# Pair sums kept in SBUF, V in P's tiles, mixed weights stored split, transfers counted by the planner

## The chip, the cores and the metric

One core of a Trainium2 chip. The metric is the device time of one execution in microseconds, the median of several runs. TensorE multiplies; VectorE (DVE), ScalarE (ACT) and GpSimd (POOL) do the elementwise work; SP issues most DMA transfers, GpSimd and ScalarE some.

## The reference

The input x has 2048 rows of 640. Two branches are mixed by a gate per row, `g = sigmoid(sum(x * gate_w))`:

```python
out = g * A(x) + (1 - g) * B(x)
# A: 32 heads of 20, 4 segments of 512 rows, causal softmax attention inside a segment,
#    plus a memory of the segments before it
for s in range(4):
    p = softmax(qs @ ks.T * scale + mask);  a_dot = p @ vs
    a_mem = (phi(qs) @ M) / (phi(qs) @ z + 1e-6)        # phi(t) = t + 1 if t > 0 else exp(t)
    o = sigmoid(beta) * a_mem + (1 - sigmoid(beta)) * a_dot
    M += phi(ks).T @ vs;  z += sum(phi(ks))
A = o @ wo
# B: a gated feed-forward layer with 1728 hidden columns
B = (silu(x @ w1) * (x @ w3)) @ w2
```

All is float32.

## The kernel before, in words

**Precision.** A float32 operand is split into a high and a low part, both in the type that TensorE multiplies at full rate; a product is three passes, high by high, high by low, low by high (`PASSES`). The function `split` makes such a pair: ScalarE casts (L194), then DVE or GpSimd subtracts (L189).

**TensorE in halves.** Most products are cut into two halves of 64 rows of the contraction, which run side by side in the array. The first halves of a product (`Work`) are issued first; at the end of them SP gets a no-operation that waits for TensorE (`w.seen`, L288), and the first matmul of the second half waits for that no-operation. So SP, which also issues transfers in order, stands in TensorE's way whenever a transfer ahead of the no-operation waits.

**The order of work is written out by a planner in the source.** `clocks` are planned TensorE times of the two halves, `busy` the planned ends of the other engines, `heap` things due later. Durations in it are constants (600 ns for a ScalarE pass, `LAND` 4200 ns for a store to land, `AGE` 5000 ns for a weight). `braid(a, b, every, skip)` runs a stream b beside a: one step of b each `every` ns of TensorE work, after `skip` ns. `segs` gives each stage of dense work and the attention slot at which it ends; attention (`attention`) runs through all stages beside the dense work.

**Stages.** The head projects Q, V and K of the first two chunks (a chunk is a segment) and writes the memory of both. Then stages of dense work beside attention: the feed-forward of pair A (chunks 0 and 1), its down products with the output projection of chunk 0; the projections of chunks 2 and 3 with the output projection of chunk 1; the feed-forward of pair B (chunks 2 and 3); its down products and the rest.

**Feed-forward of a pair.** `ffn_pair` multiplies two chunks by two weights with seven products where eight would be plain: it needs sums of blocks of x (`S`, four sums for each of two blocks k) and mixtures of the weights w1 and w3 (`mix`). `store_sums` computes the sums of both pairs in the head: it loads blocks of x into the tile `sx`, four additions each, splits each sum and stores both parts to DRAM (`sd`). `load_sums` loads them again at the pair: six into the two slots of the tag `acc` (after the memory writes that read V there; for pair B, after the third memory read and the whole output of chunk 1), two into the X tile of the second chunk. The mixtures of the weights are made once, for pair A, and stored unsplit to `md` (three per column block j, 13 blocks); pair B loads them into raw tiles (`w_load`) and splits them again (`w_split`) into the eight weight tiles `W`.

**After-steps of a product** (`after_w`, `after_3`, `after_4`) add, take tanh and multiply. They work in the product's PSUM bank where they can, so the bank is held for two or three operations.

**Tiles that matter here.** `acc`: two wide slots, first raw x, then V of chunks 0 and 1, then sums of pair A, then accumulators. `P32`: two tiles, first raw weights, then the exponentials P of attention. `hT`, `f`: rings of short-lived tiles.

**Attention.** For each pair of heads: scores (`s`), row maxima on DVE, the maxima turned and sent by GpSimd's DMA into two rows of the q tile (`row_in`, qk<-mr), then scores again with the maximum subtracted (`t`, L1491), exponentials on ScalarE (L1498), masks on GpSimd, and P times V (`o`).

Of the kernel before, what the change touches and what calls it, by code (L numbers as in the profile page):

```python
# [20 lines left out]
P = 128  # L21
# [11 lines left out]
NP, AGE = 2, 5000  # L33
# [9 lines left out]
COL, COL4, MIN_MM, APART, ISSUE, AHEAD = 0.4533, 1.7, 62, 5, 580, 1500  # L43
# [3 lines left out]
LAND, SPARE, EVEN, NOP = 4200, 99999, 0, 80  # L47
# [4 lines left out]
def gated_mix(ctx: ExitStack, tc: tile.TileContext, xT, wqk, wv, w13, w2, w2h, wo, beta, out):  # L52
# [11 lines left out]
    md = dp.tile([NF, 3, P, D], F32, name="md")  # L64
# [71 lines left out]
    busy, heap = dict(act=0.0, dve=0.0, pool=0.0, sp=0.0), []  # L136

    def now():
        return max(clocks)

# [339 lines left out]

    def slot(name):
        return cp.tile([P, 6 * L], F32, tag="acc", name=name, bufs=2)
# [34 lines left out]
    def w_load():  # L517
        k = clock["next"]
        src, n, queue, needs, *_ = items[k]
# [5 lines left out]
        if k in EARLY:  # L525
            if k % 2 == 0:
                early[:] = [sp.tile([P, 2, 1280], F32, tag="P32", name=f"wr{k}", bufs=NP)]
# [4 lines left out]
        queue.dma_start(raw[:, :n], src)  # L532
        t = go(*(("pool", ISSUE) if queue is nc.gpsimd else ("sp", 400)))
        raws.append([k, raw, n, t + AGE])
        clock["next"] += 1
        kind = items[k][6]
        if kind is not None:
            kind[1].append(raw)
            if len(kind[1]) == 2:
                for i in range(2):  # L540
                    raws.append([k + 1 + i, kind[1][i], D, t + AGE])
                clock["next"] += 2

    def w_split():
# [31 lines left out]
    def mix(w, ri, rj, j, k, done):  # L576
# [13 lines left out]
        def after():  # L590
            for i, (x, n) in enumerate(((t, 2 * P), (ri, D), (rj, D))):
                store_later(md[j, i, :, :n], x[:, :n], ("m", j, i))
# [10 lines left out]
    def w_step():  # L603
# [8 lines left out]
        if clock["next"] < min(len(items), limit() + NRAW) and landed.issuperset(items[clock["next"]][3]) and \  # L612
# [3 lines left out]
    def w_get(i):  # L616

        while i not in tiles:
# [11 lines left out]
            elif not raws or raws[-1][0] < i and clock["raws"] - len(freed) < NRAW:  # L630
# [141 lines left out]
    def store_later(dst, src, key=None, queue=nc.sync, t=None, done=None):  # L772
# [3 lines left out]
        def issue():  # L776
# [5 lines left out]
            later(go(e, 400 if e == "sp" else 330) + LAND, land)  # L782
# [142 lines left out]
    def v_blocks(c, iv, end):  # L925
# [3 lines left out]
        def begin_v():  # L929
            big["v", c] = V = slot(f"V{c}")[:, :4 * H * VE].rearrange("p (l h e) -> p l h e", l=4, e=VE)  # L930
# [182 lines left out]
    def store_sums():  # L1113

        w = cp.tile([P, KB, L], F32, tag="oall", name="sx", bufs=1)
        free_at = [0.0] * KB
        rounds = [(cs, k) for cs in ((0, 1), (2, 3)) for k in range(2)]
        loads = [(n, i) for n in range(4) for i in (2, 1, 0, 3)]
        at = {}

        def beat():
            if loads and min(free_at) <= now():
# [6 lines left out]
                store_later(w[:, slot_], xT[d, :, kb, :], ("s", n, i))  # L1129
# [22 lines left out]
        for n, (cs, k) in enumerate(rounds):  # L1152
            while not all(("s", n, i) in landed for i in range(4)):
# [12 lines left out]
            for m, o in ((2, 0), (3, 1), (1, 2), (4, 3)):  # L1166
                while not room("f", 2):
# [6 lines left out]
        selection()  # L1174

    def load_sums(cs):

        c, e = cs
        S = sums[cs] = {}

        def free_slots():
            return all((k, b) in Ms for b in range(KB) for k in cs if k < NSEG - 1) and \
                (not c or read.count(3) == 8 and all(("out", 1, q) in landed for q in range(4)))
# [4 lines left out]
        while not free_slots():  # L1188
            yield 1
        a, b = [cp.tile([P, 2, 3, L], FR, tag="acc", name=f"S{c}_{i}", bufs=2) for i in range(2)]  # L1190
        for m, k, home in ((2, 0, a[:, :, 0]), (2, 1, a[:, :, 1]), (3, 0, a[:, :, 2]), (3, 1, b[:, :, 0]), (1, 0, b[:, :, 1]), (1, 1, b[:, :, 2])):
            while ("S", cs, m, k) not in landed:
                yield 1
            load(m, k, home)
            yield 1
        while e in halves_left or not {("S", cs, 4, k) for k in range(2)} <= landed:
            yield 1
        for k in range(2):
            load(4, k, Xs[e][:, :, k])
            yield 1  # L1200
# [3 lines left out]
    def plan_pair(j, again):  # L1204

        if again:
            return [w_add(w13[2 * j], D, even=True), w_add(md[j, 0, :, :2 * P], 2 * P, even=True, needs=[("m", j, 0)]),
# [827 lines left out]
```

## Time and profile before

| | us |
|---|---|
| median of 3 runs | 1135.32 (1133.02 to 1136.27) |
| the profiled execution | 1138.12 |
| its span, first to last instruction | 1136.4 |
| TensorE busy | 1090.8 (96%) |
| DVE, ScalarE, GpSimd busy | 706.0, 563.0, 528.4 |
| mean granted TensorE clock | 0.978 |

The DMA engines moved 224.47 MB, 198 GB/s in the mean. Busy time of TensorE is the time in which at least one matmul is under way; two halves that run side by side count once, and a half that runs alone counts as busy too. A row "A <- B: total, times, longest" says that A's engine waited for B. In a chain or a timeline, `SPq` is SP's queue; the line behind it says which code issued.

### The profile page before, as it was taken

The page shows a single profiled execution, that of the slowest core. Times are in us where ns is not written, and L with a number is a line of the kernel's source. Part 1 is how long each engine was busy: PE and PEld are TensorE (multiplying, and loading weights), DVE is VectorE, ACT ScalarE, POOL GpSimd, SP SyncE. Part 2 cuts the span into 40 slices and gives each one's busy share as a digit, 9 for nine tenths or more (in the row PEclk, how much of TensorE's full clock was granted, in tenths as well). Part 3 has the DMA queues.
Part 4 walks back from the last instruction along what each step waited for, and adds up shares of the span by engine and source line. Part 5 has one row for each costly group of instructions (what it writes and reads, how often), then busy time and mean ns, then how long its engine had stood idle before and what let it go on. Part 6 is the DMA issues. An engine that isn't in the chain of part 4 may idle for free.

```text
span 1136.4 us, 29929 instructions
## 1 busy us (share of the span) xinstructions
PE 1090.8 (96%) x11369; PEld 976.3 (86%) x11369; DVE 706.0 (62%) x1932; ACT 563.0 (50%) x1158; POOL 528.4 (46%) x744
## 2 busy tenths in 40 slices
PE   9989889999999999999999998999999999999998
PEld 7978768878798899899889977878998778999998
DVE  6255457777766667575456666636767666764552
ACT  6255333554555564464766562425555545565220
POOL 3142445563446445357566573415444554545130
PEclk9999899999999999999999998969999999999999
DMA  9697795665656765556788596665576584754541
GB/s 317 223 318 273 240 348 169 185 196 166 184 173 181 215 182 162 163 151 191 233 250 274 165 316 206 194 218 154 154 197 173 140 224 120 198 150 126 170 155 48
DMA packets 145831, 224.47 MB, mean 198 GB/s; under 512 B 23148, under 2 KB 70424, under 8 KB 145688
## 3 DMA queue, kind: packets, MB, share of 16 engines
q1 hardware_dynamic: 113848, 164.73, 45.6%
q0 software_dynamic: 24064, 43.68, 15.4%
q10 hardware_dynamic: 7776, 14.16, 3.4%
q8 instruction: 90, 1.47, 0.6%
q14 instruction: 53, 0.43, 0.1%
HBM read 133.73 MB, written 87.82 MB: 195 GB/s over the span
## 4 chain that ended last, share of the span: by engine, by line
PE 77%; DMA 8%; POOL 5%; issue 4%; ACT 2%; SPq 2%; DVE 2%; POOLq 0%; DVEq 0%; ACTq 0%
PE f L285 17%; PE c L285 13%; PE z L285 6%; PE op L285 6%; PE v L285 6%; PE o L1524 6%; PE k L285 4%; PE w L285 4%; PE q L285 4%; PE t L1491 3%; PE s L1429 3%; DMA qk<-mr 3%; POOL W L189 2%; DMA sd<-S 2%; PE g L285 1%
## 5 line engine op out<-in xcount | busy, mean ns | idle before, releaser
L1440 DVE CUSTOM_DVE_ANT_0 junk<-s,mask 128x128 bf16<-128x128 f32 (+3 forms) x512 | 251.0, 490 | 138.1 <-PE s L1429 95.3
L189 POOL TENSOR_TENSOR W<-wr,W 128x640 fp32r<-128x640 f32 (+3 forms) x129 | 200.4, 1561 | 173.1 <-ACT W L194 159.4
L1498 ACT ACTIVATE P<-t 128x384 f32<-128x384 f32 (+1 forms) x384 | 180.9, 528 | 127.2 <-PE t L1491 111.2
L285 PE MATMUL c<-X,W 64*128 64x512 f32 x936 | 233.9, 399 | 0.0
L1507 POOL TENSOR_SCALAR_AFFINE_SELECT P<-P 128x256 f32<-128x256 f32 (+1 forms) x192 | 97.2, 516 | 238.6 <-ACT P L1498 212.6
L285 PE MATMUL c<-S,W 64*128 64x512 f32 x624 | 180.6, 406 | 3.3 <-DMA S<-sd 3.3
L194 ACT CAST W<-wr 128x640 fp32r<-128x640 f32 (+2 forms) x218 | 149.0, 704 | 51.7 <-PE f L285 23.4
L285 PEld LDWEIGHTS c<-X,W 64*128 64x128 f32 x936 | 155.8, 188 | 7.7 <-issue 1.4
L285 PE MATMUL f<-XW,W 64*128 64x320 f32 x1536 | 156.1, 308 | 2.6 <-SPq L288 2.6
L285 PEld LDWEIGHTS f<-XW,W 64*128 64x128 f32 x1536 | 148.2, 185 | 3.9 <-SPq L288 2.8
L285 PE MATMUL f<-W,W 64*128 64x320 f32 x1056 | 131.0, 310 | 0.2 <-SPq L288 0.2
L285 PE MATMUL w<-X,W 64*128 64x512 f32 x468 | 129.1, 396 | 0.0
L285 PE MATMUL z<-X,W 64*128 64x512 f32 x468 | 128.9, 396 | 0.0
L285 PEld LDWEIGHTS c<-S,W 64*128 64x128 f32 x624 | 116.1, 190 | 8.7 <-DMA S<-sd 3.7
L1491 PE MATMUL t<-qk 62*128 62x256 f32 (+2 forms) x512 | 108.0, 336 | 11.6 <-DMA qk<-mr 8.9
L285 PEld LDWEIGHTS f<-W,W 64*128 64x128 f32 x1056 | 113.5, 185 | 1.7 <-issue 0.6
L285 PE MATMUL k<-X,W 64*128 64x512 f32 x600 | 114.2, 412 | 0.4 <-SPq L288 0.4
L1429 PE MATMUL s<-qk 60*128 60x256 f32 (+2 forms) x512 | 107.2, 331 | 3.3 <-DMA qk<-qkd 1.3
L285 PE MATMUL q<-X,W 64*128 64x512 f32 x480 | 90.5, 413 | 6.4 <-SPq L288 6.4
L285 PE MATMUL op<-W,oT 64*128 64x320 f32 x960 | 93.7, 308 | 0.5 <-DVE oT L189 0.4
L285 PE MATMUL v<-W,X 64*128 64x322 f32 (+2 forms) x948 | 92.8, 309 | 0.1
L285 PEld LDWEIGHTS op<-W,oT 64*128 64x128 f32 x960 | 88.9, 185 | 2.1 <-DVE oT L189 1.3
(157 smaller groups left out, 2153.8 us busy)
## 6 DMA issues: line engine op xcount, KB each, us to landing
qk<-qkd POOLq DMA_DIRECT2D x128, 240.0 KB, 4.9
wr<-in_w_dram SPq DMA_DIRECT2D x69, 320.0 KB
hd<-H SPq DMA_DIRECT2D x26, 512.0 KB
qkd<-qs SPq DMA_DIRECT2D x20, 512.0 KB
qkd<-ks SPq DMA_DIRECT2D x20, 512.0 KB
wr<-hd SPq DMA_DIRECT2D x32, 320.0 KB
md<-wr SPq DMA_DIRECT2D x26, 320.0 KB
wr<-md SPq DMA_DIRECT2D x26, 320.0 KB
```

What stands on the lines that cost most here:

```text
L189: return lambda: e.tensor_sub(dst[:, 1], src, dst[:, 0].bitcast(F32))
L194: stages(bank, ("act", ns, lambda: nc.scalar.copy(dst[:, 0], src)), low, done=done)
L285: ins = nc.tensor.matmul(o, l, x, start=not w.more and i == 0 and (r == 0 or not w.todo[0]), stop=i == len(todo) - 1 and (r == 1 or not w. ...
L1429: nc.tensor.matmul(ps[i][:, o:o + n], q[:, qb * P:(qb + 1) * P], k[:, :n], start=qb != 1, stop=qb != 0, skip_group_check=True)
L1440: nc.vector.tensor_tensor_reduce(out=junk[:, :n], in0=ps[i][:, o:o + n], in1=mask[:, L - n:], scale=1.0, scalar=-3.0e38, op0=ALU.add, op1= ...
L1491: nc.tensor.matmul(ps[i][:, o:o + L - q0], k[:, kb * P:(kb + 1) * P], q[:, q0:], start=kb != 2, stop=kb != 3, skip_group_check=True)
L1498: nc.scalar.activation(u["P"][:, i, o:o + n], ps[i][:, b:b + n], AF.Exp, scale=SCALE)
L1507: nc.gpsimd.affine_select(d, d, pattern=[[0, 2], [0, n], [1, P]], base=0, channel_multiplier=-1, compare_op=ALU.is_ge, fill=0.0)
L1524: nc.tensor.matmul(ps[32 * i:32 * i + 32, kb * P:], heads[2 * p + i]["v"][:, kb], pairs[p + i // 2]["P"][:, i % 2, o:o + n], start=kb == 0 ...
```

## The change

- **Pair A's sums in place.** `store_sums` runs once for each pair. For pair A it runs in the head, beside V and K, and splits sums 1 to 3 of both blocks straight into the two `acc` slots; only sum 4 goes through DRAM. For pair B it runs beside the last down products of pair A, and all sums go through DRAM as before. `load_sums` of pair B waits for each slot alone: the first after the third memory read, the second after the output of chunk 1. Sum 4's loads are cut by part and not by block.
- **V in P's tiles.** V of chunks 0 and 1 takes the `P32` tiles.
- **Two mixed weights stored split** (`WHOLE`): of the three mixtures the two wide ones are split for pair A as before, and the split pair is stored, 640 KB and not 320; pair B loads it straight into a `W` tile, with no cast and no subtraction.
- **Transfers queued in the planner's clock** (`moved`, `RATE` 320 bytes per ns): each planned landing is at least when the bytes ahead of it have passed. The row transfer is planned at 3800 ns and not 2700.
- **Other after-steps in pair B** (`SOFT`): the sum goes into an SBUF tile, so the bank is free after the first operation (the second in `after_4`); the last multiplication goes to DVE or GpSimd.
- **Stages shifted:** other spacings in `braid`, other stage ends, `AHEAD` 500 and not 1500, `gates` after the first job of the head.

```diff
+NP, AGE, WHOLE, SOFT = 2, 5000, (1, 2), ((2, 0), (2, 1), (2, 2))
-COL, COL4, MIN_MM, APART, ISSUE, AHEAD = 0.4533, 1.7, 62, 5, 580, 1500
+COL, COL4, MIN_MM, APART, ISSUE, AHEAD = 0.4533, 1.7, 62, 5, 580, 500
-    md = dp.tile([NF, 3, P, D], F32, name="md")
+    md = dp.tile([NF, 3, P, 2 * D], F32, name="md")
...
+    def moved(ap, since=None):
+        n = 4
+        for x in ap.shape:
+            n *= x
+        busy["dma"] = max(busy["dma"], now()) + n / RATE
+        return busy["dma"] + 2500
...
+    def p_tile(name, n=2560):
+        t = sp.tile([P, 4 * H * VE], F32, tag="P32", name=name, bufs=NP)
+        return t[:, :n].rearrange("p (h n) -> p h n", h=2)
...
     def w_load():
+        if kind == "whole":
+            w = sp.tile([P, 2, D + 2], FR, tag="W", name=f"W{k}", bufs=NW)
+            halfway.add(k)
+            dst = w[:, :, :n].bitcast(F32)
+            queue.dma_start(dst, src)
+            later(max(go("sp", 400) + AGE, moved(dst)), lambda: (tiles.__setitem__(k, w), halfway.remove(k)))
+            clock["next"] += 1
+            return
...
         def done():
             tiles[k] = w
+            if kind is not None and kind - 1 in WHOLE:
+                store_later(md[items[k][6][2], kind - 1].rearrange("p (a n) -> p a n", a=2), w[:, :, :D].bitcast(F32), ("m", items[k][6][2], kind - 1))
...
+        if clock["next"] < len(items) and items[clock["next"]][6] == "whole":
+            if clock["next"] < limit() and landed.issuperset(items[clock["next"]][3]):
+                w_load()
...
-            big["v", c] = V = slot(f"V{c}")[:, :4 * H * VE].rearrange("p (l h e) -> p l h e", l=4, e=VE)
+            big["v", c] = V = (slot(f"V{c}")[:, :4 * H * VE] if c > 1 else p_tile(f"V{c}", 4 * H * VE).rearrange("p h n -> p (h n)")).rearrange(
+                "p (l h e) -> p l h e", l=4, e=VE)
...
+    SUMS = (((2, 0), (2, 1), (3, 0)), ((3, 1), (1, 0), (1, 1)))
-    def store_sums():
+    def store_sums(cs, first):
+        if first:
+            S = sums[cs] = {}
+            homes = [cp.tile([P, 3, 2, L], FR, tag="acc", name=f"S{cs[0]}_{i}", bufs=2) for i in range(2)]
+            homes = {mk: homes[i][:, n] for i, three in enumerate(SUMS) for n, mk in enumerate(three)}
...
+                if first and m < 4:
+                    def here_(m=m, k=k, n=n, o=o):
+                        S[m, k] = homes[m, k]
+                        free_at[at[n, o]] = now()
+                    split(homes[m, k], x[o], None, 600, here_, spare=EVEN)
...
+        def free_slot(i):
+            return all(("out", 1, q) in landed for q in range(4)) if i else read.count(3) == 8
...
+                if (c, 0) in SOFT:
+                    stages(bank, ("dve", 690, lambda: nc.vector.tensor_add(u, u, ps), True),
+                           ("act", 600, lambda: nc.scalar.activation(t, u, AF.Tanh, scale=0.5)),
+                           ("both", 690, lambda: nc.vector.scalar_tensor_tensor(t, t, 1.0, u, op0=ALU.add, op1=ALU.mult)),
+                           done=lambda: (let(name("a")), ready.add("r")))
...
-        later(t + 2700, lambda: u.update({"in": u.get("in", 0) + 1}))
+        later(max(t + 3800, moved(src) - 500), lambda: u.update({"in": u.get("in", 0) + 1}))
...
-    head += [braid(chain([v1] + jobs_k(A) + job_q(A, 2)), presums, 400, 0, False)]
+    head += [braid(chain([v0, v1] + jobs_k(A) + job_q(A, 2)), (0, store_sums(A, True)), 300)]
...
-    seg = [braid(braid(braid(chain(q + [half, up]), chain([(0, load_sums(A))]), 400, 0), presums, 400, 0), job_read(1), 3800, 11000)]
+    seg = [braid(braid(chain(q + [half, up]), chain([(0, load_sums(A))]), 400, 0), job_read(1), 4400, 17000)]
...
-    seg = [braid(chain([d0, d1]), o1, 1400, 3000), o2, (0, load_raw(2)), braid(chain([d1b, d2]), xs, 2700, 3400, False)]
+    seg = [braid(chain([d0, d1]), o1, 300, 3000), o2, (0, load_raw(2)), braid(braid(chain([d1b, d2]), (0, store_sums(B, False)), 1500, 0), xs, 2700, 3400, False)]
...
-    segs.append((2 * H - 3, seg))
+    segs.append((2 * H - 5, seg))
...
-    segs.append((3 * H + 8, seg))
+    segs.append((3 * H + 9, seg))
```

The spacings of the later stages change likewise (job_read of chunk 2 from 2000 to 2900, of chunk 3 from 2000 and 2400 to 1700, 3200, 3600 and 3300, the output projections from 1800, 1200, 2400 and 1400 to 900, 900, 4200 and 3200).

More of the change, by code (lines that the diff above doesn't have):

```diff
@@ L526, in w_load @@
             if k % 2 == 0:
-                early[:] = [sp.tile([P, 2, 1280], F32, tag="P32", name=f"wr{k}", bufs=NP)]
+                early[:] = [p_tile(f"wr{k}")]
             raw = early[0][:, k % 2]
@@ L532, in w_load @@
         queue.dma_start(raw[:, :n], src)
[L533 to L534 removed]
+        t = max(go(*(("pool", ISSUE) if queue is nc.gpsimd else ("sp", 400))) + AGE, moved(raw[:, :n]))
+        raws.append([k, raw, n, t])
         clock["next"] += 1
@@ L629, in w_get @@
                 clocks[0] = now()
-            elif not raws or raws[-1][0] < i and clock["raws"] - len(freed) < NRAW:
+            elif clock["next"] <= i and (not raws or items[clock["next"]][6] == "whole" or clock["raws"] - len(freed) < NRAW):
                 w_load()
@@ L1152, in store_sums @@
         for n, (cs, k) in enumerate(rounds):
-            while not all(("s", n, i) in landed for i in range(4)):
+            while not all(("s", cs, n, i) in landed for i in range(4)):
                 yield beat()
@@ L1406, in load_pair @@
             go("pool", ISSUE)
+            moved(qkd[c][RH * (h + i):RH * (h + i + 1)])
         if h % 8 == 0:
@@ L1485, in t_unit @@
         if t == 0:
-            u["P"] = sp.tile([P, 2, 1280], F32, tag="P32", name=f"P{p}", bufs=NP)
+            u["P"] = p_tile(f"P{p}")
         banks, ps = zip(*[bank_tile(f"t{p}_{t}_{i}") for i in range(2)])
@@ L1935, in gated_mix @@
     o1, o2 = jobs_oproj(3)
-    tail = [braid(chain([d1b, d2]), o1, 1400, 6000), o2]
+    tail = [braid(chain([d1b, d2]), o1, 3200, 0), o2]
     def at_job(n):
```

88 lines of the change are left out of this document (51 added, 37 removed).

## The prediction

> **What bounds the kernel now.** I read the page's busy lines first, then the busy table cut at the kernel's stages, then TensorE's waits.
>
> ```profile
> span 1136.4 us, 29929 instructions
> PE 1090.8 (96%) x11369; PEld 976.3 (86%) x11369; DVE 706.0 (62%) x1932; ACT 563.0 (50%) x1158; POOL 528.4 (46%) x744
> ```
> The table by stage has the window, its length, the busy time and count of TensorE, weight loads, DVE, ScalarE and GpSimd, the granted clock, the DMA share and GB/s:
> ```profile
> 75.00:175.00 100.00, 84.26 (x742) 74.51 (x740) 53.46 (x109) 40.39 (x80) 37.60 (x58) 0.91 0.86 294
> 175.00:375.00 200.00, 196.97 (x1820) 172.58 (x1817) 147.51 (x435) 104.75 (x216) 104.16 (x149) 1.00 0.60 174
> 375.00:550.00 175.00, 172.19 (x2181) 160.12 (x2180) 113.50 (x329) 94.45 (x193) 92.02 (x125) 1.00 0.64 186
> ...
> 675.00:760.00 85.00, 78.10 (x688) 63.87 (x687) 47.67 (x148) 31.33 (x69) 32.38 (x50) 0.86 0.74 231
> 760.00:980.00 220.00, 211.75 (x1961) 186.74 (x1961) 155.74 (x451) 118.55 (x246) 108.70 (x155) 0.99 0.60 163
> ```
> And TensorE's waits: total us, times, longest.
> ```profile
> PE t L1491 <- DMA qk<-mr: 8.9, 7, 2.6
> PE q L285 <- SPq L288: 6.4, 3, 5.6
> PE pm L285 <- SPq L288: 3.5, 2, 3.3
> PE c L285 <- DMA S<-sd: 3.3, 1, 3.3
> ...
> PE pm L285 <- ACT pkn L1003: 2.7, 1, 2.7
> PE gt L283 <- DMA gm<-gd: 2.3, 2, 1.3
> PE pkt L283 <- SPq L288: 2.1, 2, 1.1
> ```
>
> TensorE is the bound: its matmuls are 96% busy, no other engine is above 62%, and these stages have it 96% busy or more, except two. From 75 to 175 us (the head: K projections, memory of pair A, pair sums) it idles 100 - 84.26 = 15.7 us at a granted clock of 0.91, and there the DMA engines are 0.86 busy, the most of any row. From 675 to 760 us (opening of pair B) it idles 6.9 us at 0.86. Between 175 and 375 us it idles 3.0 of 200 us at 1.00, so 1.5% is what a good stage costs. A change that touches DVE, ScalarE or GpSimd alone moves nothing here; one that takes away idle TensorE time gains that time and the slow clock behind it.
>
> **Step 1, sums of pair A in place; sums of pair B moved out of the head.** The head's waits are named SPq L288: the second row half's first matmul waits for a no-operation on SP, and SP had transfers ahead of it. The rows show whose: the longest gap, the chain through it, and the head's transfers.
>
> ```profile
> 145.92 3.90 PE L285 MATMUL q<-X,W 64*128 64x512 f32 x19 [5.62 <-SPq L288]
> ```
> ```profile
> 137.78 10.74 DMA sd<-S
> ```
> ```profile
> ACT qs L794 <- DMA qkd<-qs: 13.5, 1, 13.5
> ```
> ```profile
> DMA packets 16078, 29.37 MB, mean 294 GB/s; under 512 B 1525, under 2 KB 3068, under 8 KB 16069
> ...
> S<-sd SPq DMA_DIRECT2D x6, 512.0 KB
> sd<-sx SPq DMA_DIRECT2D x11, 256.0 KB
> sd<-S SPq DMA_DIRECT2D x10, 256.0 KB
> ...
> sx<-in_xT_dram SPq DMA_DIRECT2D x7, 256.0 KB
> ```
>
> In this stretch the sums issue 21 stores (5.5 MB), 6 loads of S (3.1 MB) and 7 loads of x (1.8 MB). The change keeps pair A's sums 1 to 3 in the two wide slots: the 6 loads go, and of pair A's second round (5 of the stores here, the other 16 are pair B's) only sum 4's 2 stores stay. Pair B's 16 stores and its x loads go to the stage after 375 us. That is 19 x 0.262 + 3.1 + 1.8 = 9.9 MB less. Three mixed pairs store wider weights here (+6 x 0.328 = 2.0 MB), so 7.9 MB net leave, 27 us of transfers at 294 GB/s. SP also sheds 32 issues, and ScalarE's 13.5 us wait for a q tile's store is a wait for the same queue.
>
> Gain: the three SPq rows give 6.4 + 3.5 + 2.1 = 12.0 us. The 2.7 us behind pkn is the memory's own chain and stays. The clock costs 0.09 x 84.26 = 7.6 us of the busy time; I let it go in proportion to the idle time, 12.0/15.7, which is 5.8. Sum -18 us. Ends: 0 (SP is still late, behind the qkd stores), and -22 (idle down to the 1.5 us of a good stage, 14.2, plus all 7.6).
>
> The price is that V of chunks 0 and 1 lies in the two P32 tiles, so the first two P tiles wait for the last memory write. Its last matmul and the first t matmul in TensorE's timeline:
>
> ```profile
> 131.73 0.28 PE L285 MATMUL pm<-V,pkn 64*128 64x147 f32 x1
> ...
> 179.70 0.59 PE L1491 MATMUL t<-qk 62*128 62x512 f32 x2 [1.07 <-DMA qk<-mr]
> ```
>
> Both move forward together, so these 48 us hide it and I cost it at nothing; were that cover gone, it would cost what V is late.
>
> **Step 2, pair B's sums in the stage from 375 to 550 us.** Eight x loads, 16 stores, and this work:
>
> ```profile
> L1141 DVE TENSOR_TENSOR sx<-sx,S 128x512 fp32r<-128x512 f32 x14 | 13.1, 979 | 3.1 <-ACT S L1150 3.1
> ```
> ```profile
> PE f L285 <- SPq L288: 2.8, 2, 2.6
> ```
>
> Pair B's half lands here: 8 casts on ScalarE, and 8 subtractions and 8 additions of that size at 0.98 us, 16 us, on DVE (or GpSimd), beside 94 and 114 busy of 175, and 24 x 0.262 = 6.3 MB at a DMA share of 0.64. Engines have room; SP does not always, since this stage's only TensorE wait (last row, from the waits of this window) is again SP's. 24 issues more join that queue. Nearest row for a bad end: the head's 12.0 + 5.8 us with both pairs' 32 stores, half of which is 9. For a good end: 0. I take +3, nearer the good end, as the share here is 0.64 and not 0.86.
>
> **Step 3, opening of pair B.** SP's timeline and the wait of 3.3 us above:
>
> ```profile
> 711.62 2.14 SPq L780 DMA_DIRECT2D gd<-gm  x2
> ...
> 730.97 2.47 SPq L780 DMA_DIRECT2D S<-sd  x3
> ```
>
> The loads of S start at 730.97 because all six wait for the output of chunk 1; the last memory read left at 711.62. Now the first three need that read alone and can start some 15 us earlier, so sums 2 (and half of 3) are there before the pair's second product. The 3.3 us go, and with them about half of the clock loss of this row (0.14 x 78 = 11 us; the other half I leave to the gm waits of the same stage): -8.8. Against it, the first two pairs' wide weights bring 4 x 0.328 = 1.3 MB into the same stretch, 5.7 us of transfers at 231 GB/s, of which I charge half: net -6. Ends 0 and -12 (both 3.3 and 2.3 us of waits and 6 of the clock).
>
> **Step 4, mixed weights stored split, loaded whole.** In pair B 26 casts and 26 subtractions go, 26 loads of 320 KB become 640 KB, as do 26 stores in pair A's stage.
>
> ```profile
> L194 ACT CAST W<-wr 128x640 fp32r<-128x640 f32 x37 | 26.1, 734 | 0.0
> L189 POOL TENSOR_TENSOR W<-wr,W 128x640 fp32r<-128x640 f32 x24 | 37.8, 1587 | 36.3 <-ACT W L194 32.0 <-PE s L1429 3.6
> L189 DVE TENSOR_TENSOR W<-wr,W 128x640 fp32r<-128x640 f32 x13 | 12.2, 939 | 0.0
> ```
> ```profile
> L532 SPq DMA_DIRECT2D wr<-md x39: 319/325/1503, 682.6 to 926.0; - x39
> ```
> ```profile
> 760.37 12.51 SPq L532 DMA_DIRECT2D wr<-md  x2
> ```
>
> ScalarE loses 26 x 0.734 = 19 us and GpSimd up to 41 us between 760 and 980 us; both were half idle, so nothing comes of it directly. The load now writes the W tile itself, so SP waits until TensorE has read that slot's last weight; behind it stand the no-operations that TensorE waits for. An issue is 0.325 us: 26 x 0.325 = 8.5 us at the worst, 0 if the slot is free in time (the planner issues it only once the slot is counted free, about one pair of 16 us ahead). I take +1. The 8.5 MB of extra stores and as many of loads meet a share of 0.60: bounds 0 and +4, I take +1.
>
> **Step 5, banks freed sooner, transfers timed, stages shifted.** In pair B three of the after-steps add into an SBUF tile, so the bank is free after one operation and not two or three; no TensorE wait on a bank shows, so 0. The planner now counts bytes at 320 B/ns and gives the row transfer 3.8 us, not 2.7. In pair B's stage TensorE waits for it:
>
> ```profile
> PE t L1491 <- DMA qk<-mr: 6.4, 4, 2.6
> ```
>
> 1.1 us more per transfer, and the slot for dense work this opens, covers four waits of 1.6 us in the mean for two thirds: -4. Ends 0 and -8 (the row and the clock). New braid spacings, AHEAD and stage ends have no row; the idle times of the good stages (3.0 us from 175, 2.8 from 375) say there is little to win and as much to lose: 0, ends -5 and +8.
>
> A rule speaks against the after-steps. The row first: a subtraction with both inputs in SBUF took 939 ns for 640 columns, 1.47 ns each. The Trainium skill, SBUF — State Buffer, section "Who interferes with whom", says that a DVE instruction with two SBUF inputs contends with a GpSimd instruction that reads SBUF, and that the loser is blocked for the whole instruction. By that rule 39 operations, 27 us at 0.69 us each, newly close the port to GpSimd, and the sum below would be -23 + 27 = +4 if all of it lay on the path; I leave it a small chance, since GpSimd is busy 108.70 of 220 us and sheds up to 41.
>
> **Sum.** -18 + 3 - 6 + 1 + 1 - 4 = -23 us. The profiled execution took 1138.12 us (span 1136.4 and 1.7 around it), 2.8 above the median of the runs, 1135.32; I take the difference as it is: 1135.3 - 23 = 1112 us. Ends of the terms together: -47 and +29.5; they won't all fall on one side.
>
> **Rivals.**
> (a) The head is held by the memory chain (k, feature, transpose, copy, write) and not by the queue. For it: the 2.7 us behind pkn, and ScalarE copies that wait for TensorE; against it: 12.0 of 15.7 us carry SP's name. Step 1 then gives a third, -6: sum -11, 1124 us.
> (b) The head's gain returns: pair B's sums reach the SP queue in the middle (+9), and the S loads still wait because the third memory read moved later (step 3: +3, the wide weights alone). -18 + 9 + 3 + 2 = -4, with row transfers as before; with half of step 1, +5. About 1135 us: no change.
> (c) All idle goes: -22 in the head, -12 at the opening, -8 in pair B, +3 and +2: -37, 1098 us.
> (d) Slower, by one mechanism: the whole-weight loads hold SP. SP showed 12.51 us on two md loads at 760 us (step 4), and that was for a raw buffer. If each of the 26 waits 1 us for its slot, 26 us go and the change is level; from there on it loses. At 2 us each, -24 + 52 = +28: 1163 us. Against it: the slot is counted free before the issue.
> (e) The port rule above, all on the path: +4, 1139 us.
>
> **Chances.** The forecast (1104 to 1119 us) 0.45; (a) 0.20; (c) 0.12; (b) 0.11; (d) 0.08; (e) 0.04. Under 0.3% (3.4 us) a measurement of this kernel can hardly tell from no change. Faster is the forecast, (a) and (c): 0.77; same is (b): 0.11; slower is (d) and (e): 0.12. The range from 1094 to 1134 us leaves out (d), (e) and part of (b); the forecast alone would have 1104 to 1119.
>
> **What would show it.** Right: between 75 us and the first t matmul TensorE's SPq L288 waits fall under 4 us, the clock is above 0.96, the first t matmul starts before 165 us (now 179.70); no S load of pair A is left but X<-sd; S loads of pair B start in two groups; casts L194 of 640 columns drop by 26. Wrong: t waits that grow, a P tile that waits for pm, SP rows of md loads of a microsecond and more, or new SPq waits between 375 and 550 us.

## The result, and the profile after

The changed kernel took 1121.66 us (median of 4 runs, 1117.15 to 1123.92) against 1134.68 for the kernel before on the same chip: ratio 0.988, 95% interval 0.9846 to 0.9915. That is 1.2% faster, by 13 us. The forecast was 1112, with a range from 1094 to 1134. The profiled execution took 1121.1 us.

The page's first lines of the changed kernel, the span and TensorE's busy time:

```profile
span 1119.4 us, 29837 instructions
PE 1079.0 (96%) x11369; PEld 967.2 (86%) x11369; DVE 697.0 (62%) x1914; ACT 546.9 (49%) x1132; POOL 508.0 (45%) x736
```

The busy table of the changed kernel in the windows used before (window, length, busy time and count of TensorE, weight loads, DVE, ScalarE, GpSimd, then granted clock, DMA share, GB/s):

```profile
75.00:175.00 100.00, 100.00 (x974) 93.78 (x972) 58.39 (x155) 47.99 (x98) 33.38 (x60) 1.00 0.72 244
175.00:375.00 200.00, 195.86 (x1875) 172.56 (x1873) 145.55 (x416) 106.92 (x220) 103.11 (x149) 1.00 0.72 216
375.00:550.00 175.00, 168.17 (x2085) 156.12 (x2082) 119.27 (x319) 96.48 (x198) 89.45 (x118) 1.00 0.69 208
675.00:760.00 85.00, 77.80 (x708) 66.47 (x706) 44.98 (x145) 29.15 (x67) 24.09 (x44) 0.90 0.62 202
760.00:980.00 220.00, 209.04 (x1996) 180.82 (x1995) 148.37 (x435) 107.68 (x229) 102.25 (x154) 0.98 0.70 201
```

The head is full: 100.00 of 100 us busy at clock 1.00, where it was 84.26 at 0.91. In every other window TensorE is busy a little less than before, and the DMA share rose from 0.60 to 0.70 and more in the two long ones. TensorE's waits over the whole execution (total us, times, longest) say the same:

```profile
PE t L1555 <- DMA qk<-mr: 13.5, 9, 2.8
PE c L293 <- SPq L296: 6.6, 2, 6.4
PE s L1493 <- DMA qk<-qkd: 4.3, 5, 1.5
PE f L293 <- SPq L296: 3.3, 3, 1.8
...
PE gt L291 <- DMA gm<-gd: 2.1, 1, 2.1
...
PE k L293 <- SPq L296: 0.9, 2, 0.6
PE pkt L291 <- SPq L296: 0.8, 1, 0.8
```

The q and pm waits on SP of the head are gone (between 75 and 155 us none is left; k 0.9 and pkt 0.8 lie elsewhere). But `c <- DMA S<-sd` of 3.3 us has become `c <- SPq` with 6.4 us in one piece, and the waits for row transfers (`qk<-mr`) and q tiles (`qk<-qkd`) have grown. In the changed kernel's lines, L293 is the matmul, L296 the no-operation on SP, L806 a queued store or load, L552 a raw load and L536 a whole weight's load.

Windows at fixed times mix stages once these have moved, so the ledger goes by the first matmul of each stage, read from the timelines. Here c, w and z are products of a pair's feed-forward, f its down products and op the output projection. Lengths in us; the last column is the span of that execution:

| stage | to first c of pair A (head) | to first op of chunk 0 (pair A) | to first op of chunk 1 (middle) | to first c of pair B | to first z (opening) | to first f (pair B) | to the end | span |
|---|---|---|---|---|---|---|---|---|
| before | 154.0 | 286.0 | 255.0 | 33.5 | 23.2 | 223.5 | 161.2 | 1136.4 |
| after | 131.5 | 283.0 | 261.2 | 32.5 | 24.9 | 226.3 | 160.0 | 1119.4 |
| e1_sums_only | 130.3 | 286.8 | 258.4 | 38.1 | 20.1 | 222.7 | 165.3 | 1121.7 |
| e2_b_in_head | 145.1 | 281.4 | 258.1 | 35.5 | 21.8 | 220.9 | 161.6 | 1124.4 |
| e3_unsplit | 132.1 | 277.6 | 260.8 | 35.5 | 21.6 | 224.8 | 161.7 | 1114.1 |
| e5_u_wide_stores | 131.6 | 285.1 | 258.0 | 37.1 | 15.5 | 222.6 | 159.5 | 1109.4 |
| e9_late_wide | 131.1 | 285.8 | 259.6 | 36.0 | 16.2 | 222.7 | 159.9 | 1111.3 |
| e10_early_wide | 131.5 | 277.7 | 261.6 | 34.1 | 24.9 | 222.8 | 161.1 | 1113.7 |
| e7_u_spacing_old | 131.6 | 286.1 | 261.8 | 34.5 | 23.8 | 218.7 | 164.4 | 1120.9 |
| e12_u_ahead | 131.7 | 278.1 | 259.0 | 33.5 | 16.8 | 219.4 | 161.5 | 1100.0 |

The profiled execution of e3_unsplit, 1115.85 us, is the slowest of its runs and 6.6 us above their median, so its row is not a typical one. From before to after the span falls by 17.0 us, more than the medians do, since the profiled execution of before lies 3.4 us above its median and that of after 0.6 below: head -22.5, pair A -3.0, middle +6.2, opening +1.7, pair B +2.8, the two others -2.2. So beyond the head the stages together lost 5.5 us.

### The profile page after: what moved, and what is told of

The parts are those of the page before. It is cut to its first block, busy times and chain, and to the rows that moved or that the text cites. A ratio compares the mean times of both kernels' runs of the same rounds, so it can differ in the third digit from the quotient of the medians.

```text
span 1119.4 us, 29837 instructions
## 1 busy us (share of the span) xinstructions
PE 1079.0 (96%) x11369; PEld 967.2 (86%) x11369; DVE 697.0 (62%) x1914; ACT 546.9 (49%) x1132; POOL 508.0 (45%) x736
## 4 chain that ended last, share of the span: by engine, by line
PE 74%; DMA 10%; POOL 6%; issue 5%; DVE 2%; ACT 1%; SPq 1%; POOLq 0%; DVEq 0%; ACTq 0%
PE f L293 17%; PE c L293 13%; PE op L293 7%; PE z L293 6%; DMA qk<-mr 5%; PE o L1588 4%; PE k L293 4%; PE v L293 4%; PE w L293 4%; PE q L293 3%; PE t L1555 3%; PE s L1493 3%; DMA qk<-qkd 2%; PE g L293 1%; PE q L897 1%
## 5 line engine op out<-in xcount | busy, mean ns | idle before, releaser
L293 PE MATMUL c<-X,W 64*128 64x512 f32 x936 | 231.1, 399 | 0.3 <-SPq L296 0.3
L197 POOL TENSOR_TENSOR W<-wr,W 128x640 fp32r<-128x640 f32 (+3 forms) x106 | 163.6, 1552 | 108.9 <-ACT W L202 102.8
L293 PE MATMUL c<-S,W 64*128 64x512 f32 x624 | 181.6, 403 | 6.4 <-SPq L296 6.4
L293 PEld LDWEIGHTS c<-X,W 64*128 64x128 f32 x936 | 154.7, 188 | 9.5 <-SPq L296 1.0
L293 PE MATMUL f<-XW,W 64*128 64x320 f32 x1536 | 157.3, 308 | 3.3 <-SPq L296 3.3
L202 ACT CAST W<-wr 128x640 fp32r<-128x640 f32 (+3 forms) x192 | 130.8, 698 | 59.8 <-PE f L293 26.8
L293 PEld LDWEIGHTS f<-XW,W 64*128 64x128 f32 x1536 | 148.6, 185 | 5.0 <-SPq L296 4.1
L293 PE MATMUL f<-W,W 64*128 64x320 f32 x1056 | 136.0, 310 | 0.0
L293 PE MATMUL w<-X,W 64*128 64x512 f32 x468 | 130.5, 402 | 0.3 <-SPq L296 0.3
L293 PE MATMUL z<-X,W 64*128 64x512 f32 x468 | 128.9, 394 | 0.0
L293 PEld LDWEIGHTS c<-S,W 64*128 64x128 f32 x624 | 114.5, 189 | 12.8 <-SPq L296 6.8
L1555 PE MATMUL t<-qk 62*128 62x256 f32 (+2 forms) x512 | 103.7, 334 | 15.2 <-DMA qk<-mr 13.5
L293 PEld LDWEIGHTS f<-W,W 64*128 64x128 f32 x1056 | 116.3, 185 | 1.3 <-issue 0.8
L293 PE MATMUL k<-X,W 64*128 64x512 f32 x600 | 114.3, 403 | 0.9 <-SPq L296 0.9
L1493 PE MATMUL s<-qk 60*128 60x256 f32 (+2 forms) x512 | 103.2, 331 | 4.3 <-DMA qk<-qkd 4.3
L293 PE MATMUL v<-W,X 64*128 64x320 f32 (+2 forms) x948 | 93.8, 310 | 0.4 <-DVE gm L935 0.4
L293 PE MATMUL op<-W,oT 64*128 64x320 f32 x960 | 92.0, 308 | 0.9 <-ACT oT L202 0.4
L293 PEld LDWEIGHTS w<-X,W 64*128 64x128 f32 x468 | 87.0, 190 | 4.0 <-SPq L296 0.7
L293 PEld LDWEIGHTS v<-W,X 64*128 64x128 f32 (+1 forms) x948 | 88.9, 185 | 1.4 <-issue 1.2
```

The source lines that it names most:

```text
L197: return lambda: e.tensor_sub(dst[:, 1], src, dst[:, 0].bitcast(F32))
L202: stages(bank, ("act", ns, lambda: nc.scalar.copy(dst[:, 0], src)), low, done=done)
L293: ins = nc.tensor.matmul(o, l, x, start=not w.more and i == 0 and (r == 0 or not w.todo[0]), stop=i == len(todo) - 1 and (r == 1 or not w. ...
L1493: nc.tensor.matmul(ps[i][:, o:o + n], q[:, qb * P:(qb + 1) * P], k[:, :n], start=qb != 1, stop=qb != 0, skip_group_check=True)
L1555: nc.tensor.matmul(ps[i][:, o:o + L - q0], k[:, kb * P:(kb + 1) * P], q[:, q0:], start=kb != 2, stop=kb != 3, skip_group_check=True)
```

## Experiments

Medians, with the ratio to the kernel before on the same chip and its 95% interval. The kernel before took 1134.36 to 1135.64 us on these chips, and by the intervals a difference between two of the versions below is good to 4 to 6 us.

**e1_sums_only: the sums alone.** Everything but the new places of sums and V is set back:

```diff
-NP, AGE, WHOLE, SOFT = 2, 5000, (1, 2), ((2, 0), (2, 1), (2, 2))
+NP, AGE, WHOLE, SOFT = 2, 5000, (), ()
-        return busy["dma"] + 2500
+        return 0.0
...
# and AHEAD 1500, the row transfer at 2700, the old spacings and stage ends
```

> The changed kernel with only the pair sums changed (pair A's in place, V in P's tiles, pair B's sums beside the down products); weights stored unsplit, old after-steps, the planner's old clock, AHEAD and spacings. Theory: the sums alone shorten the head, so the first t matmul starts at 155 to 160 us (179.70 before, 155.0 after), SPq L288 waits ahead of it are under 4 us, and the median is 1113 to 1123 us. Rival: the planner's clock and the spacings made the head shorter; then the first t matmul starts after 168 us and the median is above 1127 us.

Measured: 1123.36 us, ratio 0.990 (0.9868 to 0.9933). First c of pair A at 130.3 us, TensorE 99.76 busy of 75 to 175 at clock 1.00. The sums alone make the head: the first t matmul starts at 152.5 us, even earlier than the theory had it, though the time lies just above its range. With the old spacings the first part of the middle, from the first op of chunk 0 to V of chunk 2, takes 104.5 us where before had 96.0 and after has 98.0.

**e2_b_in_head: pair B's sums back in the head.**

```diff
-    head += [braid(chain([v0, v1] + jobs_k(A) + job_q(A, 2)), (0, store_sums(A, True)), 300)]
+    presums = chain([(0, store_sums(A, True)), (0, store_sums(B, False))])
+    presums = presums[0], iter(presums[1])
+    head += [braid(chain([v0, v1] + jobs_k(A) + job_q(A, 2)), presums, 300, 0, False)]
```

> The changed kernel with pair B's sums back in the head, behind pair A's. Theory: half of the head's gain is pair B's 16 stores and 8 loads of x; the first t matmul starts at 165 to 175 us and the stage from 375 us gets about 3 us back: 1125 to 1133 us. Rival: keeping pair A's sums in place is enough, since no loads of S are left in SP's queue; the first t matmul starts before 159 us, and without the sums in the middle stage the kernel is as fast or faster: 1115 to 1121 us.

Measured: 1129.68 us, ratio 0.9949 (0.9929 to 0.9969). First c of pair A at 145.1: 13.6 of the 22.5 us of the head are given back. Its busy row of 75 to 175 us, and its TensorE waits there:

```profile
75.00:175.00 100.00, 93.17 (x909) 87.73 (x907) 59.27 (x134) 48.52 (x95) 31.27 (x51) 0.98 0.78 270
```
```profile
PE pm L293 <- SPq L296: 6.7, 2, 3.5
```

The waits that come back carry SP's name, at the places where the kernel before had them (pm). The 2.7 us behind `pkn` do not. So the head was held by the transfers and not, as in rival (a), by the memory's chain; and pair B's 16 stores and 8 loads of x are more than half of it. In the middle their move costs 3 to 5 us: 261.2 against 258.1 in all, 98.0 against 93.1 up to V of chunk 2.

**e3_unsplit: the mixed weights unsplit again.**

```diff
-NP, AGE, WHOLE, SOFT = 2, 5000, (1, 2), ((2, 0), (2, 1), (2, 2))
+NP, AGE, WHOLE, SOFT = 2, 5000, (), ((2, 0), (2, 1), (2, 2))
```

> The changed kernel with the mixed weights stored unsplit, cast and subtracted again in pair B. Theory: the wide weights fill the opening of pair B (4 x 0.33 MB of 12 MB); the 6.35 us gap there falls under 4 us and the rest of pair B stays within 2 us: 1116 to 1120 us. Rival: the relief of ScalarE (26 casts, 19 us) and GpSimd (26 subtractions, 41 us) is what holds pair B's stage where it is; without it the stage is 4 us or more longer: 1125 us or more.

Measured: 1109.26 us, ratio 0.977 (0.9734 to 0.9806), 12.4 us faster than with the wide weights. That is below the range of its theory; the gap did fall under 4 us (3.1). The wide weights relieve the engines as forecast, but the time shows nothing of it: without the relief pair B's stage takes 224.8 us, with it 226.3. ScalarE's casts of this line before and after:

```profile
L194 ACT CAST W<-wr x218: 401/728/777, 16.3 to 1106.3; 128x640 fp32r<-128x640 f32 x80, 128x256 fp32r<-128x256 f32 x13, 128x642 fp32r<-128x642 f32 x8, 128x512 fp32r<-128x512 f32 x8
```
```profile
L202 ACT CAST W<-wr x192: 399/727/762, 15.8 to 1089.4; 128x640 fp32r<-128x640 f32 x148, 128x512 fp32r<-128x512 f32 x16, 128x642 fp32r<-128x642 f32 x15, 128x256 fp32r<-128x256 f32 x13
```

218 less 192 is the 26 casts foreseen. What the transfers cost instead, the next experiments part.

**e5_u_wide_stores: the wide stores without the wide loads.** Unsplit weights as in e3, but the split pair is stored besides, to a place nobody reads:

```diff
+                store_later(mw[items[k][6][2], kind - 1].rearrange("p (a n) -> p a n", a=2), w[:, :, :D].bitcast(F32), ("mw", items[k][6][2], kind - 1))
```

> The unsplit kernel (1109.3 us), which also stores the two split mixed weights of each pair to a place that nothing reads: the wide stores of pair A's stage alone, 17 MB (pair B keeps unsplit weights, and their stores of 8.5 MB stay beside). Theory: the wide weights cost by bytes, on both sides; the stores alone lengthen pair A's stage (223 us long from the first c to the first f product in the changed kernel, 217 in the unsplit one) to 222 us or more: 1113 to 1119 us. Rival: the stores are hidden and the cost lies with the loads, which wait on SP for a weight tile; then pair A's stage stays at 219 us or less: 1107 to 1111 us.

Measured: 1111.08 us, ratio 0.9779 (0.9752 to 0.9805), 1.8 above e3, although it stores 8.5 MB more than the change. The theory was right about pair A's stage, which does grow, 285.1 against 277.6; the rival was right about the time. The opening of pair B, 15.5 against 21.6, gives most of it back in the two profiled executions, of which e3's is a slow one. From here to the change it is 10.6 us, and that leaves the loads.

**e9_late_wide and e10_early_wide: wide weights for the late or the early column blocks alone.** The tests for `WHOLE` ask `whole(j)` instead:

```diff
+    def whole(j):
+        return WHOLE if j > 1 else ()      # e9_late_wide; j < 2 in e10_early_wide
```

> The changed kernel with the first two of pair B's 13 weight pairs stored and loaded unsplit, the other 11 split as in the change. Theory: the wide loads cost mostly at the opening of pair B, where they stand in SP's queue with the sums; without the four of them there the gap of 6.35 us and the slow clock behind it go, and 7 to 9 us of the 12 come back: 1111 to 1115 us. Rival: each of the 26 wide loads costs alike; then 22/26 of the 12 us stay: 1118 to 1122 us.

> The changed kernel with only the first two of pair B's weight pairs stored and loaded split, the other 11 unsplit. Theory: the four wide loads at the opening bring back most of the loss against the unsplit kernel (1109.3 us), with a gap ahead of the first product by the sums and a clock under 0.9 behind it: 1114 to 1120 us. Rival: the loss is spread over pair B: 1108 to 1112 us.

Measured: e9_late_wide 1110.86 (ratio 0.9779, 0.9754 to 0.9803), e10_early_wide 1115.24 (0.9828, 0.9803 to 0.9854). Leaving out the first four wide weights of 26 wins 10.8 of the 12.4 us; those four alone cost 6.0. The gap is as each theory had it, and e9's time lies just below its theory's range, e10's inside it. TensorE's timeline at the first `c<-S,W` matmul, behind its idle time, in the changed kernel, in e10_early_wide and in e9_late_wide (there the no-operation is L299):

```profile
725.07 0.79 PE L293 MATMUL c<-S,W 64*128 64x512 f32 x1 [6.35 <-SPq L296]
...
726.09 0.62 PE L293 MATMUL c<-S,W 64*128 64x512 f32 x1
```
```profile
721.76 0.79 PE L296 MATMUL c<-S,W 64*128 64x512 f32 x1 [6.43 <-SPq L299]
```
```profile
723.96 0.50 PE L296 MATMUL c<-S,W 64*128 64x512 f32 x1 [0.92 <-SPq L299]
...
724.30 0.39 PE L296 MATMUL c<-S,W 64*128 64x512 f32 x1
```

With the four early loads the wait is over 6 us and the matmuls behind it take 0.62 us each; without them it is 0.92 and they take 0.39. The Trainium skill, TensorE: Matmul & The Clock Gate, section "Part 1: The HAM clock gate", says that the clock falls to half after an idle window of about 3.4 us; the rows agree that it falls after 6.35 and 6.43 us and not after 0.92. But other traces here show the granted clock at 0.50 behind shorter waits at this place, 3.30 us in the kernel before, 2.3 in e1 and 1.5 in e12, so 3.4 us is no bound here. The opening takes 24.9 us in the change and in e10, 16.2 in e9 and 15.5 in e5. By the record of the granted clock TensorE is at 0.50 there for 17.1 us in the change and in e10, 13.7 in e3, 10.2 in e1 and 3.4 in e12, and not at all in e9 and e5; the kernel before had 17.1 us as well. The queue behind the wait, in SP's timeline of the changed kernel (start, duration, line):

```profile
704.66 0.34 SPq L552 DMA_DIRECT2D wr<-in_w_dram  x1
705.10 0.39 SPq L552 DMA_DIRECT2D wr<-md  x1
710.33 0.53 SPq L536 DMA_DIRECT2D W<-md  x1
711.12 1.33 SPq L806 DMA_DIRECT2D S<-sd  x3
712.66 1.24 SPq L806 DMA_DIRECT2D X<-sd  x1
714.00 0.42 SPq L806 DMA_DIRECT2D qkd<-ks  x1
714.68 0.53 SPq L536 DMA_DIRECT2D W<-md  x1
715.31 1.58 SPq L806 DMA_DIRECT2D qkd<-ks  x1
719.19 0.36 SPq L806 DMA_DIRECT2D X<-sd  x1
720.66 0.35 SPq L552 DMA_DIRECT2D wr<-in_w_dram  x1
721.97 1.81 SPq L806 DMA_DIRECT2D hd<-ft  x2
724.62 0.34 SPq L552 DMA_DIRECT2D wr<-md  x1
```

and the chain of the changed kernel that ends at that matmul:

```profile
712.66 11.94 DMA X<-sd
724.62 0.34 SPq L552
...
725.07 1.43 PE c L293 x4
```

The issues stall at 714.68, 719.19, 723.16 (the second `hd<-ft`) and 724.62. Each started within 0.02 us of the landing of the transfer eight issues ahead of it: the raw load of 704.66, `W<-md` of 710.33, `S<-sd` of 712.03 (the last of three), `X<-sd` of 712.66. The last raw load, at 724.62, has nothing to do with that X tile; it stood behind an 11.94 us transfer, the no-operation stood behind it, and TensorE behind the no-operation. In the changed kernel the DMA engines are full meanwhile: busy rows from 700 to 725 us of the changed kernel and of e9_late_wide,

```profile
700.00:725.00 25.00, 18.71 (x150) 16.47 (x146) 13.33 (x39) 8.45 (x19) 5.03 (x10) 0.90 1.04 357
```
```profile
700.00:725.00 25.00, 24.08 (x215) 20.00 (x213) 16.70 (x50) 11.42 (x24) 10.39 (x18) 1.00 0.94 297
```

357 GB/s at a share of 1.04 against 297 at 0.94; counted from 8 us ahead of the first c in both, it is 357 against 324 at 0.98. The early wide loads put 1.3 MB more into the 25 us in which the sums come. In e9 the load that stood eight issues ahead of the last one before the no-operation took less:

```profile
714.92 8.00 DMA S<-sd
```

That the transfers are slow because too many come at once fits these rows; no run changed the bytes and left the order of the issues as it was.

**e4_s_on_act: the sums of pair B loaded through ScalarE's queue**, the change otherwise whole:

```diff
-                            t=now(), done=lambda i=i: i and
+                            queue=nc.scalar, t=now(), done=lambda i=i: i and
```

> The changed kernel with pair B's eight loads of sums (and pair A's two loads of sum 4) issued from ScalarE's queue and not from SP's; nothing else is moved by hand. Theory: at the opening of pair B SP issues no transfer before the one eight places ahead has landed, so the no-operation behind them comes late; with eight issues less on SP the gap of 6.35 us at 718 us falls under 2.5 us and the clock behind it stays at 1.00: 1113 to 1118 us. Rival: the DMA engines are full there (357 GB/s) and the sums themselves come late; TensorE waits as long, only by another name: 1120 to 1124 us.

Measured: 1122.37 us, ratio 0.9893 (0.986 to 0.9925): no better than the change. The wait is 5.8 us instead of 6.4. The chain of this kernel:

```profile
713.65 0.44 ACTq L806
714.10 0.04 issue
714.14 12.01 DMA S<-sd
726.15 0.02 issue
726.16 0.62 SPq L806
```

An issue on SP waited for a load that ScalarE had issued, and that load stood eight issues ahead when both queues are counted together. So the rival was right: another queue gets no more out of full DMA engines, and the eight places are shared.

**e8_u_softoff: the after-steps as before**, on e3:

```diff
-NP, AGE, WHOLE, SOFT = 2, 5000, (), ((2, 0), (2, 1), (2, 2))
+NP, AGE, WHOLE, SOFT = 2, 5000, (), ()
```

> The unsplit kernel with the old after-steps in pair B. Theory: no TensorE wait on a bank showed before, so the banks freed sooner are worth under 3 us: 1108 to 1112 us. Rival: the planner opens the next product sooner where a bank is free, so pair B's stage (246 us from its first c to the first f product behind it in the unsplit kernel) grows by 4 us or more: 1114 to 1119 us.

Measured: 1110.76 us, ratio 0.9777 (0.9749 to 0.9805), 1.5 above e3 with intervals that overlap. The after-steps cost nothing that can be seen, so the 27 us of blocked port of rival (e) are not on the path. The port rule stands in the Trainium skill, SBUF — State Buffer, section "Who interferes with whom"; no time by it is seen here.

**e6_u_clockoff and e11_u_rowold: the planner's clock**, on e3. In e6 `moved` returns 0 and the row transfer is planned at 2700 ns; in e11 the bytes are still counted and only the row goes back:

```diff
-        return busy["dma"] + 2500
+        return 0.0
-        later(max(t + 3800, moved(src) - 500), lambda: u.update({"in": u.get("in", 0) + 1}))
+        later(t + 2700, lambda: u.update({"in": u.get("in", 0) + 1}))
```

> The unsplit kernel with the planner's old clock (landings not counted by bytes, row transfer 2.7 us). Theory: of the 14.1 us between the sums alone and the unsplit kernel the clock carries most, since transfers that are planned to land too early make TensorE wait: 1117 to 1124 us, and t and s matmuls wait 3 us more for qk transfers than the 9.8 us there. Rival: the spacings carry it; then 1108 to 1112 us and the same waits.

> The unsplit kernel (1109.3 us) with the row transfer planned at 2.7 us again; landings are still counted by bytes. Theory: it is the row's 3.8 us that cost the 4.9 us between the unsplit kernel and the one with the old clock (1104.4), since t products are held back for a transfer that is mostly there: 1103 to 1107 us. Rival: counting bytes costs them, by putting off stores and loads: 1108 to 1112 us.

Measured: e6 1104.43 (ratio 0.9735, 0.9705 to 0.9765), e11 1116.33 (0.983, 0.9803 to 0.9857). TensorE's waits for the row in pair B's stage, 730 to 1000 us, of the changed kernel, of e3, of e6 and of e11; before had 6.4, 4, 2.6:

```profile
PE t L1555 <- DMA qk<-mr: 7.9, 6, 2.8
```
```profile
PE t L1555 <- DMA qk<-mr: 6.5, 6, 2.2
```
```profile
PE t L1555 <- DMA qk<-mr: 3.9, 5, 1.5
```
```profile
PE t L1555 <- DMA qk<-mr: 8.0, 6, 1.9
```

The waits are not shorter with the new clock than without it. Beyond that nothing is settled: 4.9 us better without the clock, where the intervals of e3 and e6 overlap, and 7.1 worse with half of it. With the old spacings the clock won nothing either: e7 below has it and took 1125.15 us, e1 has not and took 1123.36 (e1 has the old after-steps besides). Both e6 and e11 fell outside the ranges of theory and rival.

**e7_u_spacing_old and e12_u_ahead: spacings and AHEAD**, on e3. AHEAD is the lead, in planned time, that the second halves may have over the first halves (ns). e12 sets only AHEAD back to 1500; e7 sets AHEAD and all spacings and stage ends back:

```diff
-COL, COL4, MIN_MM, APART, ISSUE, AHEAD = 0.4533, 1.7, 62, 5, 580, 500
+COL, COL4, MIN_MM, APART, ISSUE, AHEAD = 0.4533, 1.7, 62, 5, 580, 1500
...
-    seg = [braid(braid(braid(chain(q), r, 2900, 11000), o1, 900, 15000, False), r3, 1700, 75000, False)]
+    seg = [braid(braid(braid(chain(q), r, 2000, 4000), o1, 1800, 20000, False), r3, 2000, 60000, False)]
```

> The unsplit kernel with the old spacings, stage ends and AHEAD of 1500 ns. Theory: the spacings carry under a third of the 14.1 us: 1109 to 1114 us. Rival: they carry most, by placing pair B's sums, the memory reads and the output projections where SP and the DMA engines are free: 1117 to 1124 us, with the second V projection starting 8 us or more later than the 507.8 us of the unsplit kernel.

> The unsplit kernel with AHEAD back at 1500 ns and the new spacings and stage ends. Theory: of the 15.9 us that old spacings and AHEAD cost together, the spacings carry most, since the loss stood in the stage with pair B's sums (from the first output product to the second V projection 107.5 us, 98.1 in the unsplit kernel): 1108 to 1113 us. Rival: AHEAD carries it, because second halves that run 1.5 us ahead leave first halves alone in the array: 1117 us or more.

Measured: e7 1125.15 (ratio 0.9919, 0.9888 to 0.995), e12 1101.65 (0.9696, 0.9674 to 0.9718). So the spacings and stage ends alone are worth 1125.15 - 1101.65 = 23.5 us here, and AHEAD 500 costs 1109.26 - 1101.65 = 7.6. e7 is as its rival had it, a little beyond the range; e12 is faster than either of its ranges. Of the 23.5, pair A's stage has 8.0 and the opening 7.0 (stage table). e12, the change without its wide weights and with AHEAD as it was, is the fastest version measured, 20.0 us under the change.

## Why the prediction was right or wrong

Faster was right, and the time lay in the range; the 1112 was 9.7 us too low, and the narrower band of the forecast alone, 1104 to 1119, was missed by 2.7. The time came closer to rival (a)'s 1124, but (a)'s mechanism did not occur: the head gained more than forecast, and the rest lost it elsewhere.

**Step 1 (-18): right, just beyond its good end.** The head is 22.5 us shorter (end -22). All its signs came: no wait on SP is left between 75 and 155 us, clock 1.00, first t matmul at 155.0 (179.70 before), and no sum of pair A loaded but `X<-sd`. e1 shows the sums do it alone, e2 that pair B's share of the transfers is 13.6 us of it. One row was misread: the chain with `sd<-S` of 137.78 lasts to 148.52 us, past the end of the longest gap at 145.92, and leads to a wait of 0.38 us at 151.55. What held the longest gap stands in SP's timeline of the kernel before:

```profile
132.31 5.37 SPq L780 DMA_DIRECT2D S<-sd  x6
...
142.81 3.00 SPq L780 DMA_DIRECT2D qkd<-qs  x2
```

The two issues of the second row waited 2.45 and 2.24 us, for the `S<-sd` loads of 133.83 and 134.55, and the no-operation stood behind them. So it was pair A's loads of S that ended this gap late, by the same wait for the eighth issue back as at the opening of pair B; the change takes them out too, so the term stands. Another detail of the working was off: 75 to 175 us moved 24.4 MB and not 29.4 - 7.9 = 21.5. And V in P's tiles cost nothing to be seen: no P tile waited for pm.

**Step 2 (+3, ends 0 and +9): right in size.** The middle grew by 6.2 us, 2.0 of it up to V of chunk 2. The nearest row, SP's wait at f, went from 2.8 to 3.3 us. But with the old spacings (e1) the first part grows by 8.5, the bad end; the +2.0 needs the new spacings, which step 5 had at nothing.

**Step 3 (-6): wrong in sign.** The loads of S did split into two groups, at 700.50 and 711.12 us, both earlier than before (730.97). The step took an earlier issue for an earlier landing. The loads met the whole weights, the last memory read's transfers and the K and q tiles in 25 us at 357 GB/s, X<-sd took 11.94 us, and an idle time of 3.3 us became one of 6.35. I had charged these weights half of 5.7 us of transfer time, as if only the bytes counted; what counted was which issue stood behind the slow transfer. Without the early wide weights (e9) the opening takes 16.2 us against 23.2 before: a gain of 7, with the late wide weights still there. With no wide weights and the new spacings it takes 21.6 (e3, the slow execution), 21.3 (e11), 19.7 (e8), 18.7 (e6) and 16.8 us (e12). So a gain of 2 to 7 us was there, and the early wide weights of step 4 took it.

**Step 4 (+2): the mis-sized term; it measured +12.4** (interval of the two ratios together: roughly 7 to 18). Loads 10.6, stores 1.8, by e5. The place is not that of the working: no whole load held SP (longest issue 0.571 us in the group row below, and none started more than 0.26 us after SP's instruction ahead of it), so rival (d) did not occur.

```profile
L536 SPq DMA_DIRECT2D W<-md x26: 518/530/571, 702.4 to 930.0; - x26
```

An issue took 0.530 us in the median, not 0.325. The stores' bound of +4 was broken inside pair A's stage, which under the new spacings takes 283.0 to 285.8 us with all of them or all but four (after, e5, e9) and 277.6 to 278.1 without the late ones (e3, e10, e12). Early loads alone cost 6.0, all but the early 1.6. That is less than 12.4 together, but each of the three is good to 5 us or so, so it is not shown that they fail to add up. The stage table would have a reason, an opening that is 5 to 6 us shorter in e9 and e5 than in e3 and returns what the stores cost; but e3's row is from its slowest execution, and no run tested it alone.

**Step 5 (0, -4, 0): one right, two wrong.** The after-steps are nothing (e8). The clock's -4 did not come: the row waits of pair B went from 6.4 to 7.9 us. The spacings' 0 (ends -5 and +8) is the largest miss, hidden in the sum: -23.5 without AHEAD, +7.6 for AHEAD. I argued from idle times of 3 us in good stages that there was little to win. The gain was not in the idle time of before: with the old spacings pair A's stage stays at 286.1 us and the opening at 23.8, with the new ones they shrink to 278.1 and 16.8. Which of the spacings does it was not tried.

**The sum.** Put together from the runs in this order: steps 1 to 3 with the old spacings -12.2 (e1, beside 1135.56 of the kernel before on that chip) where the terms had -21; step 5 -14.1 (e1 to e3) where they had -4; step 4 +12.4 (e3 to the change) where they had +2. That is -13.9 for -23: two misses of 9 and 10 us one way and one of 10 the other. That the time still lay in the range is in part luck: one miss made up for another, and the range was 40 us wide. In e1 rival (b) is half true: of 23.7 us won in the head, 3.4 came back in the middle, 4.6 ahead of pair B's first c and 4.1 at the end. Rival (c), all idle gone, did not occur. The shares depend on each other, so this ledger holds only in this order.

## What to carry to other kernels

Idle time that the trace puts down to a queue went here when the transfers in that queue went, and the granted clock came back with it; this could be forecast from the rows. Trading engine work for DMA bytes where engines have slack was a loss at the place where the DMA engines were already near full, and a mean share over a stage (0.60) did not show that place: look for the 25 us in which the bytes meet. Of a hand-planned order, price the constants by runs; the profile of before did not price them.

## What the runs showed of the hardware

A DMA issue on SP can wait for the landing of the transfer eight issues earlier, whether or not it depends on it. The instruction records of the traces show what sets the eight. Each issue names the semaphore that its landing raises, and SP's and ScalarE's issues use eight of these between them, in turn. The stalled issue waits for the semaphore that it will raise itself: `wr<-md` at 724.62 us waits for number 101, which the `X<-sd` of 712.66 has yet to raise. So the wait is an instruction of the built program, not a limit that the DMA queue showed. In the changed kernel 19 issues of SP were let go by the landing of a transfer of these two queues: 17 of them in this way, each exactly eight issues behind, and two that read what the transfer had written. In e4 it is 17 of 20, in the kernel before 14 of 19. Such a wait makes one 11.94 us load stop TensorE for 6.35 us through an unrelated load.

The 640 KB loads were issued in 0.530 us in the median, where the raw `wr<-md` loads of up to 320 KB took 0.325 in the kernel before. Size alone does not set this time: `hd<-ft`, 128 KB, took 0.633 us in the changed kernel.
